# Shaking the due times of a list scheduler in a fused attention and MLP-mixer kernel

## The chip, the cores and the metric

The kernel runs on one core of a Trainium2 chip. The metric is the time of one execution in device microseconds (us). Before the change it is 423.1 us (median of 3 runs). Each experiment is timed beside the kernel before on the same chip.

## The reference

Eight batches of eight heads, 1024 positions, head size 64. Keys and values are first projected from 1024 positions to 64 (Linformer), then comes attention, then a token mixer with a residual and a channel mixer with a residual.

```python
k_proj = einsum('ks,bhsd->bhkd', E, k);  v_proj = einsum('ks,bhsd->bhkd', F, v)
attn = softmax(q @ k_proj.T / sqrt(64));  x = attn @ v_proj        # -> (8, 1024, 512)
h = relu(x.T @ w_tok1) @ w_tok2;          u = x + h.T              # 1024 -> 256 -> 1024
out = u + relu(u @ w_ch1) @ w_ch2                                  # 512 -> 1536 -> 512
```

## The kernel before

The kernel does not issue instructions as it goes. It records 2222 units of work ("jobs", each a few instructions of one engine or one transfer) with their dependencies, an estimated duration and a due time, and a list scheduler in the kernel's own code puts them in order and assigns the eight PSUM banks (the buffers that TensorE writes its products to). The program is then emitted in that order. So a due time decides only the order, not when something runs. The core of the scheduler:

```python
def plan(self):
    ...                                        # due times from those of the users
    for g in self.groups:                      # jobs that have to stay in sequence
        first = min(j.prio for j in g)
        for n, j in enumerate(g):
            j.prio = first + 0.01 * n
    ...
    while any(can.values()):
        ...                                    # for each engine: the jobs that can start
            t0 = min(c[0] for c in cands) + 0.02
            c = min((c for c in cands if c[0] <= t0), key=lambda c: (c[1], c[2]))   # due first
        ...
    return sorted(order, key=lambda j: j.at)
```

Transfers are on this schedule too, as jobs of one engine "DMA" that does one at a time, with a fixed duration. In the program GpSimd issues nearly all loads and stores, SyncE the transposes. A transpose of `u` (SBUF to SBUF, for the channel mixer) is entered with 3.5 us plus 2.0 of latency; those of batches 2 and later (batches are numbered from 0) get 3.0 us more. To keep loads and transposes apart, the kernel adds waits ("ties"). For batch b, four loads of 0.5 MB each bring k and v (first and second half of the heads); the transposes that take turns with them are the two of batch b - 2 (comments added):

```python
def load_kv(b):
    first, second = turned_u.get((b - 2, 0)), turned_u.get((b - 2, 1))
    jobs = load_group(b, "kv", first)     # k, k, v, v; all wait for the first transpose of u
    if second:
        tie(second, jobs[2])              # second transpose behind the first v
        tie(jobs[3], second)              # second v behind that transpose
        rest[b] = jobs[3:]                # put in a group with the q loads: v, q, q
```

If the loads go k, k, v, the second transpose waits for all three and runs alone.

The softmax here doesn't subtract the row's maximum and nothing guards it: scores larger than these inputs give would overflow.

## Time and profile before

| | before |
|---|---|
| time, median of 3 runs | 423.1 us |
| span of the profiled run | 421.2 us |
| TensorE (PE) busy | 98% |
| VectorE / ScalarE busy | 83% / 55% |
| stops of TensorE over 0.1 us after the first 38 us | 2.8 us in all |

TensorE decides the time. A "stop" here is the start of a matmul less the start of the one before it, less the columns of that earlier one at the full pace (0.109 us for 256 columns). The prediction shows the lines and how they are read.

### The profile page before, as it was taken

How to read it: one execution, taken by the hardware profiler on the slowest of the kernel's cores; microseconds unless marked ns; L12 is line 12 of the kernel's file. 1: busy time of each engine (PE TensorE's matmuls, PEld its weight loads, DVE VectorE, ACT ScalarE, POOL GpSimd, SP SyncE). 2: the span in 40 equal slices, each digit the busy share in tenths (PEclk: the TensorE clock that was granted, in tenths of full speed). 3: DMA queues.
4: the chain of work that ended last, by engine and by line, in shares of the span. 5: the costliest groups of instructions: out<-in, count | busy, mean ns of one | idle time of the engine just before them, and what ended most of it. 6: DMA issues, size and time to landing. Idle time of an engine off the chain costs nothing.

```text
span 421.2 us, 9421 instructions
## 1 busy us (share of the span) xinstructions
PE 412.1 (98%) x3838; PEld 347.7 (83%) x3838; DVE 348.0 (83%) x747; ACT 231.8 (55%) x444; POOL 66.2 (16%) x104
## 2 busy tenths in 40 slices
PE   7999999999999999999999999999999999999996
PEld 3587877688788888888798888888898899988885
DVE  2359969679679798988889899898988798997685
ACT  1858884475636546564645556655646645354530
POOL 8453220022003030022103020212100000010110
PEclk9999999999999999999999999999999999999999
DMA  9999999996975989398974989999760501250223
GB/s 166 207 201 206 207 206 164 225 177 140 216 145 103 195 133 235 64 186 141 207 163 94 191 139 224 163 200 179 153 146 0 152 27 76 50 151 2 102 100 103
DMA packets 96668, 62.48 MB, mean 148 GB/s; under 512 B 62064, under 2 KB 92272, under 8 KB 96624
## 3 DMA queue, kind: packets, MB, share of 16 engines
q0 software_dynamic: 34944, 45.09, 54.5%
q1 hardware_dynamic: 61056, 16.00, 21.6%
q10 hardware_dynamic: 624, 0.79, 0.7%
q8 instruction: 30, 0.49, 0.5%
q14 instruction: 14, 0.11, 0.1%
HBM read 59.24 MB, written 16.78 MB: 180 GB/s over the span
## 4 chain that ended last, share of the span: by engine, by line
PE 91%; DVE 4%; ACT 2%; DMA 1%; issue 0%; DVEq 0%
PE psum L1253 34%; PE psum L1144 33%; PE psum L848 4%; PE psum L484 4%; PE psum L597 3%; PE psum L964 3%; PE psum L656 2%; DMA o<-in_F_dram 1%; PE psum L620 1%; DVE u L1071 1%; PE psum L736 1%; PE psum L687 1%; PE psum L581 1%; PE psum L405 1%; PE psum L711 1%; PE psum L1032 1%
## 5 line engine op out<-in xcount | busy, mean ns | idle before, releaser
L1253 PEld LDWEIGHTS <-G 128*128 128x128 bf16 x1344 | 130.6, 98 | 19.7 <-issue 1.5
L1253 PE MATMUL psum<-wc_sb,G 128*128 128x256 bf16 x768 | 102.5, 273 | 0.5 <-ACT psum L1309 0.2
L1166 ACT ACTIVATE G<-psum 128x512 bf16<-128x512 f32 x96 | 57.3, 600 | 56.0 <-PE psum L1144 55.4
L1144 PEld LDWEIGHTS <-wc_sb 128*128 128x128 bf16 x768 | 73.8, 98 | 10.9 <-issue 0.6
L1253 PE MATMUL psum<-wT,G 128*128 128x256 bf16 x576 | 77.7, 273 | 0.1
L1180 DVE TENSOR_TENSOR G<-G 128x512 bf16<-128x512 bf16 (+1 forms) x140 | 69.5, 516 | 1.0
L1144 PEld LDWEIGHTS <-wT 128*128 128x128 bf16 x576 | 55.7, 98 | 9.0 <-issue 1.2
L1144 PE MATMUL psum<-uT,wc_sb 128*128 128x256 bf16 x384 | 57.7, 273 | 0.2 <-ACT psum L1187 0.2
L1144 PE MATMUL psum<-S,wc_sb 128*128 128x256 bf16 x384 | 57.6, 273 | 0.1
L1144 PE MATMUL psum<-S,wT 128*128 128x256 bf16 x384 | 55.6, 273 | 0.4 <-DVE S L781 0.4
L1287 POOL DMA_DIRECT2D out_dram<-o x30 | 16.4, 548 | 240.2 <-DVE o L1293 125.6
L1125 DVE CUSTOM_DVE_ANT_0 G<-psum,ub 128x512 bf16<-128x512 f32 x48 | 32.9, 685 | 15.3 <-PE psum L1144 15.1
L1172 ACT COPY ua<-psum 128x512 f32<-128x512 f32 x48 | 28.2, 588 | 30.1 <-PE psum L1144 29.7
L606 ACT ACTIVATE a<-psum 128x512 bf16<-128x512 f32 x64 | 36.4, 602 | 12.4 <-PE psum L597 11.8
L1293 DVE TENSOR_TENSOR o<-psum,u 128x512 f32<-128x512 f32 x55 | 37.5, 683 | 6.4 <-PE psum L1253 6.3
L1187 ACT COPY psum<-psum 128x512 f32<-128x512 f32 x48 | 27.8, 580 | 18.9 <-DVE G L1125 9.9
L1125 DVE CUSTOM_DVE_ANT_0 G<-psum,ua 128x512 bf16<-128x512 f32 x48 | 32.7, 682 | 5.0 <-ACT ua L1172 4.6
L1172 ACT COPY ub<-psum 128x512 f32<-128x512 f32 x48 | 28.2, 588 | 7.0 <-PE psum L1144 6.3
L1144 PE MATMUL psum<-uT,wT 128*128 128x256 bf16 x192 | 28.8, 273 | 0.1
L673 DVE TENSOR_TENSOR x_sb<-psum,rdn 128x512 bf16<-128x512 f32 x40 | 27.4, 686 | 0.6
L597 PE MATMUL psum<-qT,kT 128*128 128x512 bf16 x64 | 21.5, 380 | 0.6 <-ACT kT L549 0.6
L346 POOL DMA_DIRECT2D v_sb<-in_v_dram x18 | 13.5, 749 | 50.7 <-DMA uT<-u 48.0
(108 smaller groups left out, 547.2 us busy)
## 6 DMA issues: line engine op xcount, KB each, us to landing
out_dram<-o POOLq DMA_DIRECT2D x30, 512.0 KB, 4.2
k_sb<-in_k_dram POOLq DMA_DIRECT2D x14, 512.0 KB, 8.5
v_sb<-in_v_dram POOLq DMA_DIRECT2D x14, 512.0 KB, 10.3
q_sb<-in_q_dram POOLq DMA_DIRECT2D x14, 512.0 KB, 9.9
wc_sb<-in_moe_w_ch_dram POOLq DMA_DIRECT2D x6, 256.0 KB, 12.3
wc_sb<-in_moe_w_ch_dram POOLq DMA_DIRECT2D x4, 384.0 KB, 12.3
k_sb<-in_k_dram POOLq DMA_DIRECT2D x4, 256.0 KB, 6.8
v_sb<-in_v_dram POOLq DMA_DIRECT2D x4, 256.0 KB, 7.3
```

Source lines behind the costliest of these rows:

```text
L484: nc.tensor.matmul(t[0:KP, 0:hn], ET_sb[:, si, :], k_sb[:, hs, si, :], start=a, stop=z)
L597: lambda: nc.tensor.matmul(bank(bk), kT[:, h].rearrange("p c k -> p (c k)"), qT[:, h].rearrange("p j s -> p (j s)"), start=True, stop=True,),
L606: lambda: nc.scalar.activation(out=a_t[h // 2 % 2][:, h % 2], in_=bank(bk), func=ACT.Exp, scale=scale),
L673: lambda: nc.vector.tensor_tensor(out=x_sb[:, :, h * D : (h + 1) * D].rearrange("p (n c) d -> p n c d", n=2), in0=view()[:, :, :, 0:D], in ...
L1125: nc.vector._custom_dve(TENSOR_ADD_SAT, out=out, in0=in0, in1=in1, s0=FMAX, s1=0.0)
L1144: nc.tensor.matmul(t[:, c, :], w1_of(n, dd, 2 * m + c), a_of(j, n, dd), start=(n in (1, 7) and c == 0 and dd == 0), stop=(c == 1 and dd == 1),
L1166: lambda: nc.scalar.activation(out=G[:, n, cs], in_=view(src), func=ACT.Relu),
L1172: 512, lambda: nc.scalar.copy(out=dst, in_=view("y")), writes=[(name, s % 2)],
L1180: 512 * len(both), lambda: f(out=G[:, n, c], in0=G[:, a, c], in1=G[:, b, c]), ps=False,
L1187: 512, lambda: nc.scalar.copy(out=view("y"), in_=view("x")), takes=[bk["y"]],
L1253: nc.tensor.matmul(to, G[:, G_OF[n], cc, t * P : (t + 1) * P], w2_of(n, cc), start=(n in opens and (t == 0 or alone) and cc == 0), stop=(c ...
L1293: 512, lambda: nc.vector.tensor_add(out=dst, in0=view(src), in1=u_of(sh, dh)),
```

## The change

Its intent is to find a better order among many nearly equal ones: each due time is shaken by up to 0.8 us either way with a fixed sequence, and among many such shaken orders the one was kept whose planned time, averaged over randomly delayed transfers, is shortest. All of it but the three constants (`SHAKEN_FROM = -30.0`, `SHAKE = 1.6`, `SEED = 2441`):

```diff
             if j.prio > 1e8:
                 j.prio = max((d.prio for d in j.deps), default=0) + 2
+
+
+        for j in self.jobs:
+            if j.prio > SHAKEN_FROM:
+                j.prio += SHAKE * ((j.n * j.n * 7919 + j.n * SEED * 31 + SEED * SEED * 17) % 10007 / 10007 - 0.5)
         free = {}
```

The shaking comes after the groups, so it can also part what a group had put in sequence. All line numbers behind the change are 8 higher: L1152 is the L1144 of before, L1261 the L1253.

## The prediction

> **What bounds the kernel now.** I read the page first (busy shares, slices, chain of work), then TensorE's waits, then TensorE's timeline around its longest stops, then SyncE's and GpSimd's timelines for the transfers. The page's first lines and its chain:
>
> ```profile
> span 421.2 us, 9421 instructions
> PE 412.1 (98%) x3838; PEld 347.7 (83%) x3838; DVE 348.0 (83%) x747; ACT 231.8 (55%) x444; POOL 66.2 (16%) x104
> PE 91%; DVE 4%; ACT 2%; DMA 1%; issue 0%; DVEq 0%
> ```
>
> The reader is to see one engine, TensorE (PE), with work from end to end, and 91% of the chain that ended last on it. No other engine is near. So only two things can move the time: more or fewer matmuls, or more or fewer stops of TensorE. TensorE's own waits, complete:
>
> ```profile
> PE psum L433 <- DMA o<-in_F_dram: 1.5, 1, 1.5
> PE psum L405 <- DVE zero L309: 1.0, 1, 1.0
> PE psum L597 <- ACT kT L549: 0.6, 2, 0.4
> PE psum L1085 <- DVE u L1071: 0.5, 1, 0.5
> PE psum L1144 <- DVE S L781: 0.4, 1, 0.4
> PE psum L1253 <- ACT psum L1309: 0.2, 1, 0.2
> PE psum L1144 <- ACT psum L1187: 0.2, 1, 0.2
> PE psum L1253 <- DVE o L1293: 0.2, 1, 0.2
> ```
>
> Columns: total us, times, longest. The first five lie in the first 36 us, which the change hardly touches. Only the last three, 0.6 us, lie later. That understates the stops, because a matmul's row is longer than the step from one to the next. TensorE's timeline shows it:
>
> ```profile
> 229.33 0.60 PE L1144 MATMUL psum<-S,wc_sb 128*128 128x256 bf16 x4
> 230.15 0.60 PE L1144 MATMUL psum<-uT,wc_sb 128*128 128x256 bf16 x4 [0.22 <-ACT psum L1187]
> ```
>
> and the chain in order of time shows the undisturbed pace:
>
> ```profile
> 341.00 1.31 PE psum L1144 x12
> ```
>
> Twelve matmuls of 256 columns in 1.31 us are 0.109 us each. Four started at 229.33 should give way at 229.77; the next began at 230.15. So the stop was 0.38 us, although the view calls 0.22 of it idle. I took this surplus (start to start, less the columns at that pace) for every matmul. From 38 us to the last matmul, the surpluses that end with a wait on another engine and exceed 0.1 us are twelve: 0.39, 0.39, 0.38, 0.27, 0.23, 0.23, 0.18, 0.17, 0.15, 0.15, 0.12, 0.12, together 2.8 us. This is all that reordering can win after the head. 2.8 of 423 is 0.7%, so 2% faster (8.5 us) is out of reach.
>
> **What the Trainium skill says.** (1) "Perfetto Trace Analysis", introduction: matmul busy time says little of the distance to the roof, because matmuls are pipelined. The trace agrees: rows average 273 ns, starts are 109 ns apart. (2) "TensorE: Matmul & The Clock Gate", section "Wait — 56ns, not 53.3ns?": warm, start to start is columns / 2.4 GHz plus about 2.5 ns, so 109.2 ns for 256 columns. The trace agrees (109). (3) The same page, "Step-by-step: what each phase is for": matmuls stay in program order, only weight loads are pulled ahead. So one matmul whose operand is late holds all behind it, as at 229.77. (4) "DMA: Bandwidth & Descriptors", "Issuing engines are not separate DMA queues": all issuers share the 16 DMA engines. The trace agrees for slices 1 to 9, where the DMA digit stays at 9 with three queues at work.
>
> **The change part by part.** It removes and adds no instruction on TensorE: both programs have 7648 TensorE rows, 26 blank warm-up matmuls among them, and the dependencies between units of work are the same. It adds to every due time above -30 a fixed offset between -0.8 and +0.8 us, and a static list scheduler then picks another order and other PSUM banks. Of 904 TensorE units 677 stand elsewhere, by 3 places on average and 31 at most; of 741 VectorE units 554, of 443 ScalarE units 270. The first 18 TensorE units and the tail (last product and stores) stand as before, so the head, where the pace is lowest, and the last 4 us are unchanged.
>
> *Short loops.* The stops come where a product fills a PSUM bank, ScalarE or VectorE reads or reseeds it, and the next product on that bank waits, with too little other TensorE work laid between. At 229.33 and at 81.31 there is 0.44 us of such work and the stop is 0.39, so a ScalarE loop needs 0.83 us. That fits its parts: the last matmul ends 0.16 after its successor could start (273 - 109), the copy takes 0.58, and 0.09 is left for signalling.
>
> ```profile
> L1187 ACT COPY psum<-psum 128x512 f32<-128x512 f32 x48 | 27.8, 580 | 18.9 <-DVE G L1125 9.9
> L1293 DVE TENSOR_TENSOR o<-psum,u 128x512 f32<-128x512 f32 x55 | 37.5, 683 | 6.4 <-PE psum L1253 6.3
> ```
>
> The VectorE loop (0.68 instead of 0.58) needs 0.95: at 97 us there is 0.78 between and the stop is 0.17. I laid the matmuls of both orders end to end at the measured pace and counted these loops from 38 us of TensorE work on. Before, 6 loops are shorter than they need, short by 0.40, 0.39, 0.17, 0.17, 0.08 and 0.08, 1.29 us in all. The five stops found at such places measure 0.39, 0.39, 0.23, 0.23 and 0.17, 1.41 us, so the count is good to a tenth. After, 2 are too short: a VectorE loop with 0.44 between (short by 0.51) and one short by 0.08, 0.59 together. Loops under 1.0 us fall from 16 to 10, under 2.0 us from 353 to 336. Gain: 1.41 - 0.59 = about 0.8 us, all of it on TensorE, which sets the end.
>
> *Stops from queues on the evicting engines.* The other 1.4 us of the twelve are not short loops: the evicting engine was busy with something else (0.38 at 173 us, 0.30 in two stops at 210 us). No count tells what the new order makes of these. With fewer tight loops I take half, so a gain of 0.7 us.
>
> *Transfers.* Here the new order can lose. From the third batch on, loads and transposes take turns: k, k, v, then a transpose of u, then v, q, q. A late second v stops TensorE at the batch's key and value projection.
>
> ```profile
> 97.20 1.79 SPq L759 DMA_TRANSPOSE uT<-u  x1
> 101.96 0.74 POOL L346 DMA_DIRECT2D v_sb<-in_v_dram  x1 [1.34 <-DMA uT<-u]
> DMA to landing us min/median/max: 5.8/5.8/5.8
> 109.73 0.40 PE L484 MATMUL psum<-k_sb,ET_sb 128*64 128x512 bf16 x1
> ```
>
> These are SyncE's timeline, GpSimd's, the answer for that one load, and TensorE's timeline. The second v lands at 101.96 + 5.8 = 107.7, and the projection starts at 109.7: 2.0 us to spare, and about the same (2.1) in two further batches. The shaken order puts the first v ahead of both k in every second batch (frees the transpose some 5 us earlier, at 2.6 us a load) and the first q ahead of the second v (costs 2.6), and in the others moves the first v up one place. Meanwhile the projections move up in TensorE's order by 3.0, 0.9, 2.2, 4.1, 5.9 and 1.5 us in batches 2 to 7. What is left to spare, by those sums, is about 0.9 us in batch 2, 1 in batch 3 (where one qT transpose now goes ahead of uT, 2 to 3 us), 2.5 in batch 4, 0.5 in batch 5, and 2 or more after. None is negative, but three are thin, and transposes now overlap with loads, which slows both. I charge 0.4 us.
>
> Sum: -0.8 - 0.7 + 0.4 = -1.1 us, 423.1 to 422.0.
>
> **The rivals.**
> 1. *Nothing comes of it.* The stops of one kind go, others of the same size come, because 677 units moved and only the simplest loops were counted. For: of 2.8 us only half is explained by loops. Against: short loops fall at every limit I tried. Time 423.0.
> 2. *A load takes the place of the waits.* A second v lands late in batch 3 or 5 by 1 to 3 us, TensorE stands still, and the later work shifts. For: 0.5 to 1 us to spare, DMA busy at 9 tenths until about 95 us. Against: TensorE has no wait on a load after the head now, and the uT transpose before the second v starts earlier. Time 423.5 to 425.
> 3. *Nearly all stops go.* Queues on ScalarE and VectorE also thin out, no load is late. Against: the one VectorE loop with 0.44. Time 421.0.
>
> **Range and chances.** The middle is 422.0; rival 3 gives the low end, 421.0; rival 2 in its mild form the high end, 423.8. The part that cannot change (the matmuls, the head and the tail) is over 99% of the time and the runs before lie within 0.5 us, so within 2% is nearly certain. Slower by 8.5 us would take a load late in batch after batch: 1%. Faster by 8.5 us: 0.5%.
>
> **What would show it.** Right: TensorE busy stays 98%; the stops at 82, 173 and 229 us are gone; a new one of about 0.5 us stands at a VectorE eviction (L1293) near 88 us, before L1253; the surpluses over 0.1 us after 38 us sum to 1.2 to 1.6 instead of 2.8; the last v of a batch lands before its L484. Wrong: a TensorE wait on k_sb, v_sb or uT, or an L484 start that follows a landing; or the surpluses still sum to 2.8, which would be rival 1. A head longer or shorter than before (first 36 us) would mean that I misread what the shaking leaves alone.

## The result, and the profile after

The changed kernel takes 428.67 us (median of 4 runs, 428.11 to 430.18) against 423.22 for the kernel before. The ratio is 1.0133, interval 1.0106 to 1.016. The prediction said 422.0, with 423.8 as its high end: a gain of 1.1 us was foreseen, and a loss of over 5 was measured.

The head and the tail are as before. The first matmul that reads S and wT (the start of the channel mixer) begins at 35.6 us (35.9 before), and from the start of the last matmul to the end 4.2 us pass (4.3 before). Between these two marks lie 386.56 us, against 381.00. So 5.56 us are lost in the steady part. The page of the changed kernel, first lines and chain:

```profile
span 426.3 us, 9396 instructions
PE 412.5 (97%) x3823; PEld 348.6 (82%) x3838; DVE 348.5 (82%) x747; ACT 231.1 (54%) x444; POOL 66.3 (16%) x104
PE 86%; DMA 7%; DVE 4%; ACT 1%; issue 1%; POOL 1%; DVEq 0%; POOLq 0%
```

TensorE has the same work (412.5 us busy; the 15 matmuls fewer are records that the trace misses, as all 3838 weight loads are there), but DMA now holds 7% of the chain, 1% before. The list of TensorE's waits has a new first line:

```profile
PE psum L1152 <- DMA uT<-u: 4.6, 1, 4.6
```

One single wait, on a transfer that no line of the list named before: a transpose of `u`. TensorE's timeline shows where, first after the change, then the same reader before it:

```profile
99.90 0.60 PE L1152 MATMUL psum<-S,wT 128*128 128x256 bf16 x4
105.07 1.04 PE L1152 MATMUL psum<-uT,wc_sb 128*128 128x256 bf16 x4 [4.57 <-DMA uT<-u]
105.89 1.49 PE L1261 MATMUL psum<-wc_sb,G 128*128 128x256 bf16 x6
107.17 1.06 PE L856 MATMUL psum<-x_sb,wt_sb 128*128 128x256 bf16 x4
```

```profile
105.06 0.60 PE L1144 MATMUL psum<-uT,wc_sb 128*128 128x256 bf16 x4
```

Four matmuls from 99.90 should end their turn at 100.34; the reader of uT starts at 105.07, so the stop is 4.73 us. In the kernel before this reader stood at 105.06. The new order brought it forward by 4.7 us (105.06 to 100.34), and its operand did not follow. Note also that the six matmuls from 105.89 take until 107.17, which is 0.21 us each instead of 0.109. The view by windows of the changed kernel tells why; the third column from the right is the granted TensorE clock:

```profile
100.00:102.00 2.00, 0.50 (x6) 0.20 (x3) 2.00 (x6) 1.18 (x3) 0.00 (x0) 1.00 1.13 307
102.00:104.00 2.00, 0.00 (x0) 0.00 (x0) 1.33 (x3) 0.00 (x0) 0.00 (x0) 0.62 1.21 134
104.00:106.00 2.00, 0.93 (x5) 0.69 (x6) 0.43 (x1) 0.00 (x0) 0.38 (x1) 0.50 0.27 60
106.00:108.00 2.00, 2.00 (x11) 1.42 (x10) 0.00 (x0) 0.57 (x1) 1.87 (x3) 0.50 0.29 30
108.00:110.00 2.00, 2.00 (x15) 1.53 (x13) 0.00 (x0) 0.26 (x1) 0.00 (x0) 0.67 1.19 189
```

While TensorE stood, its clock was halved, from 102.5 to 109.3 by the clock records. From 105.07 to 109.3 it worked at half speed, which costs half of 4.26, 2.1 us. Stop and clock make 6.9 us. The measured loss is 5.56, so the rest of the order must have gained about 1.3.

Why was the transpose late? The answers for this one transfer, after and before:

```profile
L767 SPq DMA_TRANSPOSE uT<-u x1: 7402/7402/7402, 92.7 to 92.7; - x1
DMA to landing us min/median/max: 12.4/12.4/12.4
```

```profile
L759 SPq DMA_TRANSPOSE uT<-u x1: 1794/1794/1794, 97.2 to 97.2; - x1
DMA to landing us min/median/max: 4.2/4.2/4.2
```

It was issued 4.5 us earlier than before, and it landed 3.6 us later (105.0 against 101.4): 12.4 us under way instead of 4.2, and the issue alone held SyncE for 7.4 us instead of 1.8. GpSimd's timeline, after, shows what else was under way:

```profile
87.21 0.75 POOL L354 DMA_DIRECT2D v_sb<-in_v_dram  x1 [13.63 <-PE psum L1261]
87.95 0.77 POOL L354 DMA_DIRECT2D k_sb<-in_k_dram  x1
89.06 0.75 POOL L354 DMA_DIRECT2D k_sb<-in_k_dram  x1 [0.33 <-issue]
92.03 0.55 POOL L1295 DMA_DIRECT2D out_dram<-o  x1 [2.22 <-DVE rdn L640]
95.72 0.55 POOL L1295 DMA_DIRECT2D out_dram<-o  x1 [3.14 <-DVE o L1311]
```

The shaking put v ahead of both k. The transpose waits for that v alone, so it set out beside two k loads, and the new order also made two stores of outputs ready at just that time (before: at 100.07 and 110.73). By the landings, the k loads were in at 96.1 and 100.0, the stores at 102.5 and 103.9, the transpose last.

A third thing had moved. SyncE's timeline, after, has the first transpose of `u` behind one of q:

```profile
79.51 2.19 SPq L570 DMA_TRANSPOSE qT<-q_sb  x1
81.75 3.29 SPq L767 DMA_TRANSPOSE uT<-u  x1
```

Before, that transpose of `u` went first, at 79.96, and the one of q followed. All loads of batch 3 wait for it, so the first of them set out at 87.2 us instead of 85.5.

### The profile page after: what moved, and what is told of

The parts are those of the page before. It is cut to its first block, busy times and chain, and to the rows that moved or that the text cites. A ratio compares the mean times of both kernels' runs of the same rounds, so it can differ in the third digit from the quotient of the medians.

```text
span 426.3 us, 9396 instructions
## 1 busy us (share of the span) xinstructions
PE 412.5 (97%) x3823; PEld 348.6 (82%) x3838; DVE 348.5 (82%) x747; ACT 231.1 (54%) x444; POOL 66.3 (16%) x104
## 4 chain that ended last, share of the span: by engine, by line
PE 86%; DMA 7%; DVE 4%; ACT 1%; issue 1%; POOL 1%; DVEq 0%; POOLq 0%
PE psum L1261 33%; PE psum L1152 33%; PE psum L856 4%; PE psum L972 4%; DMA uT<-u 3%; DMA q_sb<-in_q_dram 3%; PE psum L492 3%; PE psum L605 2%; PE psum L664 2%; DMA v_sb<-in_v_dram 1%; DVE u L1079 1%; PE psum L695 1%; PE psum L719 1%; PE psum L628 1%; PE psum L744 1%
## 5 line engine op out<-in xcount | busy, mean ns | idle before, releaser
L1261 PEld LDWEIGHTS <-G 128*128 128x128 bf16 x1344 | 130.9, 98 | 19.7 <-issue 0.8
L1261 PE MATMUL psum<-wc_sb,G 128*128 128x256 bf16 x768 | 103.1, 274 | 0.5 <-DVE wait L1301 0.3
L1152 PEld LDWEIGHTS <-wc_sb 128*128 128x128 bf16 x768 | 74.2, 98 | 14.5 <-DMA uT<-u 4.8
L1261 PE MATMUL psum<-wT,G 128*128 128x256 bf16 x576 | 78.1, 273 | 0.5 <-ACT G L1174 0.2
L1152 PEld LDWEIGHTS <-wT 128*128 128x128 bf16 x576 | 55.9, 98 | 9.7 <-issue 1.0
L1152 PE MATMUL psum<-uT,wc_sb 128*128 128x256 bf16 x384 | 58.2, 274 | 4.6 <-DMA uT<-u 4.6
L1152 PE MATMUL psum<-S,wc_sb 128*128 128x256 bf16 x384 | 57.8, 273 | 0.1
L1152 PE MATMUL psum<-S,wT 128*128 128x256 bf16 x384 | 55.0, 273 | 0.5 <-DVE S L789 0.4
L1152 PE MATMUL psum<-uT,wT 128*128 128x256 bf16 x192 | 29.3, 276 | 0.1
L605 PE MATMUL psum<-qT,kT 128*128 128x512 bf16 x53 | 19.6, 379 | 1.0 <-ACT kT L557 0.7
```

The costliest lines, as they stand in the source:

```text
L605: lambda: nc.tensor.matmul(bank(bk), kT[:, h].rearrange("p c k -> p (c k)"), qT[:, h].rearrange("p j s -> p (j s)"), start=True, stop=True,),
L1152: nc.tensor.matmul(t[:, c, :], w1_of(n, dd, 2 * m + c), a_of(j, n, dd), start=(n in (1, 7) and c == 0 and dd == 0), stop=(c == 1 and dd == 1),
L1261: nc.tensor.matmul(to, G[:, G_OF[n], cc, t * P : (t + 1) * P], w2_of(n, cc), start=(n in opens and (t == 0 or alone) and cc == 0), stop=(c ...
```

## The experiments

The theory ("theory 1" below): the stop takes two things together, a transpose that shares the DMA engines with loads and stores, and its reader brought forward in TensorE's order. Rivals: the order of the loads alone ("theory 2"); the reader's place alone ("theory 3"); the late second v that the prediction had feared. All edits act on the finished plan, on single jobs around the loads of batch 3, so the rest of the program stays exactly as it was (TensorE's instructions are the same, in the same order, unless said). In the diffs, `put(a, b)` moves job a to just ahead of b, `put_after(a, b)` to just behind it, and `tied[a] = b` makes a wait for b. The jobs: 657 and 658 are the k loads, 659 the first v, 660 the second v, 915 the first q, 479 and 488 the first and second transpose of `u` of batch 1, 368 and 372 the stores.

**Loads k, k, v again (a_kkv).**

```diff
     plan = pl.plan()
+    put(657, 659)
+    put(658, 659)
```

> The changed kernel with one edit: in batch 3 the first three loads are issued k, k, v as before the change instead of v, k, k; the transpose of u (second half of batch 1) still waits for that v. TensorE order and everything else are the changed kernel's. In the changed kernel that transpose was issued at 92.65, took 12.4 us (4.2 before the change) and landed at 105.02, and TensorE stood still from 100.34 to 105.07. Theory 1 (the transpose is slow because it shares the DMA engines with the two k loads and two stores that are in flight): it now starts when v lands, at about 98 to 100, beside the stores alone, takes 4 to 7 us and lands at 103 to 105, so the stop is 3 to 4.7 us: 426 to 428 us, little gained by this edit alone. Theory 2 (the order of the loads alone is at fault): the stop goes to about 1 us and the time to about 422 to 423. Theory 3 (only the earlier place of the reader in TensorE's order counts, the transfers do not): the transpose takes as long as in the changed kernel.

Measured: 426.74 us against 423.69, ratio 1.0076 (1.0053 to 1.0099), correct. The transpose was issued at 99.4, took 4.5 us, landed at 103.9, and the stop was 3.1 us. Theory 2 fails: restoring the order of the loads recovers only about 2 of 5.5 us. Theory 3 fails in part: the transpose got fast again. The time is as theory 1 said. Of the traffic blamed, though, the stores (landed at 100.6 and 101.8) slowed this transpose hardly at all, and they had not held up the v before it either: that v took 9.8 us here and 9.7 without the stores (a_kkv_late2 below). The transpose is late here because its loads set out 2.2 us later than before (87.7 against 85.5), behind the first transpose of `u`.

**Stores behind the transpose (a_late, a_kkv_late), failed.**

```diff
+    put_after(368, 488)
+    put_after(372, 368)
+    tied[job[368]] = tied[job[372]] = job[488]
```

> The changed kernel with one edit: the two stores of outputs that were issued at 92.03 and 95.72, during the transpose, now wait until the transpose has landed. The loads stay v, k, k. Theory 1 (any traffic beside it slows the transpose): it is issued at about 92 as in the changed kernel, still beside two k loads (until about 98), takes 7 to 10 us instead of 12.4 and lands at 99 to 102; the stop is 0 to 2 us, 422 to 424.5 us. Theory 2 (load order alone): the stop stays over 4 us, 428 us. Theory 3 (place of the reader alone): no change, 428 us.

> Both edits together: loads k, k, v and the two stores behind the transpose, so that it runs alone as before the change. Theory 1: it is issued at about 97.5 to 98, takes 4.2 to 4.5 us and lands at about 102; the reader stands at 100.3, so a stop of about 1.7 us remains, and no loss of clock after it (the clock in this stage stays 1.0): 423 to 424 us. Theory 3 (place of the reader): the same 1.7 us is its whole share, against the 4.7 measured. If the time stays at 428, the transfers are not the cause.

Both gave a wrong result (436.1 and 437.6 us). My edit put the second store ahead of the addition that makes its data. They say nothing about the question, and were mended by leaving 372 where it is:

**The same, mended (a_late2 with loads v, k, k; a_kkv_late2 with loads k, k, v).**

```diff
+    put_after(368, 488)
+    tied[job[368]] = tied[job[372]] = job[488]
```

> a_late mended (there the second store was placed ahead of the addition that makes its data, hence its wrong result). The changed kernel, loads v, k, k as changed, but the two stores of outputs wait until the transpose of u has landed. Theory 1 (any traffic beside the transpose slows it): it is issued at about 92.5 and shares the DMA engines with the two k loads only; it takes 7 to 10 us instead of 12.4, lands at 99 to 102, the stop before its reader at 100.3 is 0 to 1.7 us: 421.5 to 424 us. Theory 2 (load order alone is at fault): over 4 us of stop, 428 us. Theory 3 (place of the reader in TensorE's order alone): 428 us.

> a_kkv_late mended in the same way: loads k, k, v and both stores behind the transpose, so it runs alone as before the change. Theory 1: the third load lands at about 97.7, the transpose takes 4.2 to 4.5 us and lands at about 102.1; the reader stands at 100.3, so 1.7 to 1.9 us of stop remain, which is the part of the earlier reader by itself: 423 to 424 us, with the granted clock from 100 to 110 us near 1.0. In a_kkv (stores not moved) the transpose took 4.5 and landed at 103.9. If it is slower than a_kkv (426.7), the stores were not what delayed the loads there.

Measured: 429.43 us (ratio 1.0136, 1.0119 to 1.0154) and 430.98 us (1.0171, 1.0156 to 1.0186), before 423.34; both correct. The times miss what every theory said, but the traces tell more than any other run. TensorE's waits in a_late2, then the answer for its transpose:

```profile
PE psum L495 <- DMA v_sb<-in_v_dram: 4.0, 1, 4.0
PE psum L1152 <- DMA uT<-u: 0.6, 1, 0.6
```

```profile
DMA to landing us min/median/max: 8.0/8.0/8.0
```

With the stores out of the way the transpose took 8.0 us instead of 12.4, landed at 101.4, and the stop before its reader fell from 4.73 to 0.76, as theory 1 expected. But behind it a second stop of 4.2 us appeared: the second v was now queued behind two stores and a q and landed at 113.4, while the projection that needs it stood at 109.0. A late v exists in the changed kernel too, only hidden: there the second v landed at 114.9 (106.36 + 8.5) and the projection, held back by the first stop, came at 114.7. It is not independent of the first: its tie lets it set out only after the transpose has landed, and then behind a q. The size of the second stop in these two runs is not that of the changed kernel, because my edit had also put the two stores ahead of that v. In a_kkv_late2 both stops show, 3.2 and 4.6 us. So batch 3 has two late transfers, one hidden behind the other. TensorE's wait for the first of them in a_kkv_late2:

```profile
PE psum L1152 <- DMA uT<-u: 3.0, 1, 3.0
```

There the transpose ran alone and took 4.2 us, and still landed at 103.9, 3.2 us after the reader could start. So a fast transpose is not enough. An estimate of the parts, from the landings: had it landed when it did before (101.4), the reader's new place (100.3) alone would have cost about 1.1 us of the 4.73; the later loads make that 3.1 to 3.2 (a_kkv, a_kkv_late2), and the order v, k, k with its company 4.73. Theory 1 left the later loads out.

**The suspected cost in the kernel before (b_vkk).** The same move the other way round: first v ahead of both k, TensorE's order of before.

```diff
+    put(659, 657)
```

> The kernel BEFORE with one edit, the suspected cost alone: in batch 3 the first v is issued ahead of both k, so the transpose of u starts some 5 us earlier, beside the two k loads. TensorE's order is that of before, where the reader of the transposed block starts at 105.06. Theory 1 (it takes the slow transpose and the earlier reader together): the transpose is issued at about 92, takes 6 to 10 us instead of 4.2 and lands by 102; no stop, 423.0 to 424 us, same as before. Theory 2 (load order alone is at fault): a stop of several us, 426 to 428 us.

Measured: 423.07 us against 423.34, ratio 0.9984 (0.9968 to 1.0001), correct.

```profile
L759 SPq DMA_TRANSPOSE uT<-u x1: 5175/5175/5175, 92.5 to 92.5; - x1
DMA to landing us min/median/max: 7.7/7.7/7.7
```

Beside two loads the transpose takes 7.7 us here as well, but it lands at 100.3, its reader stands near 105, and nothing is lost. The load order alone is not the cause. (The stores stayed behind the transpose here; the reverse test, the changed kernel with the reader alone put back, was not run.)

**The lost clock by itself (a_warm).** Twenty blank matmuls fill the stop.

```diff
+        if j.n == 570:                  # the reader of uT
+            for _ in range(20):
+                blank(banks[5])
+            pin()
         if j.eng == "PE":
```

> The changed kernel with 20 blank matmuls of 512 columns (4.3 us at 0.216 each) put into the stop ahead of the reader, into a PSUM bank that is free there (the reader's own, which it starts anew). The transfers and the stop's end at about 105 stay. In the changed kernel the granted clock was 0.50 from 104 to 108 us, and matmuls of 256 columns started every 0.214 us until about 108.5. If the lost clock is a cost of its own (theory: 2.0 to 2.3 us of the 7), TensorE keeps its clock and the time falls to 426.2 to 426.8 us. If the half clock comes from elsewhere, the time stays at 428.7 or rises.

Measured: 428.36 us, ratio 1.0114 (1.0099 to 1.0129), correct. The windows of a_warm:

```profile
104.00:106.00 2.00, 1.62 (x10) 0.82 (x9) 0.43 (x1) 0.00 (x0) 0.00 (x0) 1.00 0.53 83
106.00:108.00 2.00, 2.00 (x21) 1.78 (x19) 0.00 (x0) 0.57 (x1) 1.88 (x3) 1.00 0.14 20
```

The clock stays at 1.00 and 21 matmuls fit in two microseconds instead of 11, so idleness did halve the clock. But the time hardly falls, and my expectation of 426.5 was wrong. TensorE, now faster, arrives at the projection earlier and waits there for the second v (1.3 us in its trace); the transpose was also 0.5 us later. The 2.1 us of half clock were real work time, but most of it lay beside the wait for that v.

**The second v alone (a_v_only).**

```diff
+    put(660, 915)
```

> The changed kernel with the second v of batch 3 ahead of the first q, nothing else. Theory: the v lands some 2.5 us earlier than in the changed kernel (114.9), but the stop before the transposed block at 100 to 105 comes first and stays at 4.7 us with its lost clock, and the v had just landed by the time the projection came: 428 to 428.7 us, no gain. Rival (the late second v is the main cost): 424 to 426 us.

Measured: 428.53 us, ratio 1.0109 (1.0092 to 1.0126), correct. As expected, no clear gain: the stop before uT's reader stays (5.5 us in this run). The rival that the second v is the main cost fails.

**Second v ahead, stores behind it, transpose left beside the k loads (a_late_v).**

```diff
+    put(660, 915)
+    put_after(368, 660)
+    put_after(372, 368)
```

> The changed kernel's loads v, k, k and the transpose behind the first v, as changed; but the second v goes ahead of the q loads, and the two stores behind it. In a_late2 the transpose so placed took 8.0 us, landed at 101.4 and left a stop of 0.8, and the second v, queued behind two stores and a q, landed at 113.4 and stopped TensorE for 4.2 us. Theory (two thin transfers, each hidden behind the other): the stop of 0.8 stays, the v lands at about 108, and the time is 422.5 to 423.5 us, though the transpose is still slow. Rival (the transpose must go first): 426 us or more.

Measured: 423.89 us, ratio 1.0003 (0.9986 to 1.0021), correct. The loss against the kernel before is gone, though the transpose still takes 8.4 us (stop 1.1 us). The time is a little above the expected 422.5 to 423.5; the trace has a new stop of 1.15 us at 124 us, on the transpose of the keys (kT): the q loads had been pushed back, and the transposes behind them too.

**The transpose first (a_turn_first).** Issue the second transpose directly behind the first, ahead of all three loads; second v ahead of the q loads, stores behind it.

```diff
+    put(488, 659)
+    tied[job[488]] = job[479]
+    for n in (657, 658, 659):
+        tied[job[n]] = job[488]
+    put(660, 915)
+    put_after(368, 660)
+    put_after(372, 368)
```

> The changed kernel, but in batch 3 the transpose of u (second half) goes directly behind that of the first half, ahead of the three loads (which then wait for it or follow in the queue), the second v goes ahead of the q loads, and the two stores go behind that v. TensorE's order is the changed kernel's. Theory 1: the transpose is issued at about 84 to 87, lands by 91, long before its reader at 100.3; no stop there and no loss of clock; the second v lands at about 104 to 105, before the projection at 108. 421 to 422 us, that is 6 to 7 us under the changed kernel and 1 to 2 under the kernel before. If the expected gain of 1 to 1.5 us from fewer short waits was not real, 423 us. If the second v lands late, a stop of 1 to 3 us before the projection.

Measured: 422.36 us (421.95 to 422.81) against 423.69, ratio 0.9967 (0.995 to 0.9985), correct. The transpose:

```profile
L767 SPq DMA_TRANSPOSE uT<-u x1: 1771/1771/1771, 87.0 to 87.0; - x1
DMA to landing us min/median/max: 4.2/4.2/4.2
```

It runs alone, lands at 91.2, and TensorE waits for no transfer in the steady part. Between the two marks named above lie 379.57 us, 7.0 less than in the changed kernel and 1.43 less than before. TensorE's order is untouched, so the transfers made the whole loss. The edit moves the transpose, the second v and the stores at once; whether the transpose first would do alone was not run.

**Control: the transpose first in the kernel before (b_first).**

```diff
+    put(488, 657)
+    tied[job[488]] = job[479]
+    for n in (657, 658, 659):
+        tied[job[n]] = job[488]
```

> Control: the kernel BEFORE with the transpose of u ahead of the three loads of batch 3, as in a_turn_first. TensorE's order is that of before, which waits for no transfer there. Theory (the gain of a_turn_first over before, 0.3%, is that of TensorE's order with fewer short waits): 423.0 to 423.8 us, ratio 0.999 to 1.002. Rival (the gain comes from the earlier transpose itself): 422.4 us, ratio 0.997.

Measured: 423.88 us against 423.34, ratio 1.0007 (0.9987 to 1.0026), correct. Its steady part is 380.87 us, that of before 381.00. An early transpose by itself is worth nothing here. The moves of the second v and of the stores were not tried in the kernel before, but its TensorE waits for no transfer after the head (the prediction shows the list), so they had no such wait to remove. What a_turn_first wins over before is then TensorE's new order.

**Two short waits less (a_best).** In a_turn_first I took 0.50 us at 88.32 and 0.42 at 114.16 for the longest short waits. One unit of other work goes into each. (The second reading was wrong: the trace misses one 512-column matmul of L744 there, 0.22 us of work, whose weight load it has. The wait was 0.20 us.)

```diff
     ...                       # as a_turn_first
+    put_after(365, 493)
+    put(744, 546)
```

> a_turn_first with two units of TensorE work moved by one place, at the two longest short waits that its trace still shows: at 88.32 (0.50 us, a VectorE eviction with 0.44 us of work in between) a product of another block goes between, and at 114.16 (0.42 us) the second half of a token product. Theory: the two waits fall to under 0.15 us, TensorE stays the bound, so the time falls by 0.6 to 0.9 us against a_turn_first's 422.4: 421.5 to 421.9, ratio to before about 0.995. If short waits do not add up on the path, it stays at 422.4.

Measured: 421.54 us (421.27 to 421.94) against 423.34, ratio 0.9952 (0.9937 to 0.9967), correct. TensorE's timeline at the first place, in a_turn_first and in a_best:

```profile
88.14 0.39 PE L628 MATMUL psum<-vb,a 128*128 128x130 bf16 x4
88.87 0.81 PE L1261 MATMUL psum<-wc_sb,G 128*128 128x256 bf16 x6 [0.34 <-DVE wait L1301]
```

```profile
88.23 0.60 PE L1152 MATMUL psum<-uT,wc_sb 128*128 128x256 bf16 x4
88.73 0.71 PE L1261 MATMUL psum<-wc_sb,G 128*128 128x256 bf16 x5
```

The gap is filled with work. Both waits are gone from the trace, but two others came up in that execution (0.32 us on a v load at 47 us, 0.24 at 89.5), and the steady part of the profiled runs is the same (379.56 and 379.57). Their spans differ by 0.5 us, all of it before the first mark (35.95 against 36.48 us), where the edit changes nothing. The two kernels ran on different chips, and their intervals overlap. So it is shown that a_best beats the kernel before, by 0.5%; that it beats a_turn_first is not shown, though the time fell where it was expected.

## Why the prediction was wrong, and where it was right

- **What bounds the kernel, and that nothing is added on TensorE: right.** Head and tail are unchanged within 0.4 us, the work is the same. (Both programs, when built, hold 3838 matmuls and 3822 weight loads.)
- **Short loops and queues, -0.8 and -0.7 us: right in their sum.** Without the wait for uT and the half clock behind it, the stops over 0.1 us after 38 us fall from 2.8 to 1.4 us (0.50, 0.27, 0.20, 0.20, 0.12, 0.10), inside the 1.2 to 1.6 foreseen. Gaps of 0.22 us that are only a 512-column matmul missing from the trace are left out or taken off. The stops at 82, 173 and 229 us are gone, and the one new VectorE stop stands where it was said to, 0.50 us at 87.4 before L1261. With the transfers repaired (a_turn_first) the steady part is 1.43 us shorter than before, against 1.5 foreseen; by the ratio of the times the gain lies between 0.6 and 2.1 us. How it splits between the two is not shown. If the 0.50 is the only loop left over 0.1 us, loops gave 0.9 and the rest 0.5, an estimate; that half of the rest would go was a guess in the prediction, and its coming near was in part luck.
- **The step that failed: "I charge 0.4 us" for transfers.** The charge turned out to be 7.0 us (changed kernel against a_turn_first); the trace shows 6.9 of it as 4.73 of standing and 2.1 of half clock. It failed in two ways. First, "What is left to spare" was worked out for one transfer and one user only, the second v and the projection. The transposed `u` has a user too. Its reader moved forward by 4.7 us, and before the change the transpose had landed only 3.6 us ahead of it (101.4 and 105.06). Second, "(frees the transpose some 5 us earlier" was booked as a gain. An earlier start beside two loads and two stores meant 12.4 us instead of 4.2, so it landed 3.6 us later, and the second v, which waits for it, set out 4.4 us later (106.36 against 101.96) where the sum for batch 3 left 1 us to spare. The sentence that transposes now overlap with loads, "which slows both", was there, but without a size; the size can be read from a_late2, b_vkk and a_late_v: 8.0, 7.7 and 8.4 us beside two loads, 12.4 with the two stores as well. For the loads the runs do not show it: the last of the three took 9.75 us beside the transpose (b_vkk) and 9.73 without it (before).
- **Rival 2 was the right family with the wrong member and size.** A transfer of batch 3 did take the place of the waits, and TensorE stood still, but the first one was uT, not v, and the time was 428.7 and not 423.5 to 425. The second v was late as well, hidden behind the first stop: it landed at 114.9, and without stop and half clock the projection would have come at about 107.8 instead of 114.7 (an estimate: 6.9 us less).
- **The clock was not in the sum at all.** The wait was taken to cost its own length. The page "TensorE: Matmul & The Clock Gate" of the Trainium skill says in "What's actually happening" that the clock halves after an idle window of about 3.4 us. The trace agrees in the length of the window (half clock from 102.5 to 109.33, which is twice 3.41 us), but not in the idleness: TensorE had stood for only 2.2 us when the clock fell. In the end the clock cost little: with it kept (a_warm) the steady part is 0.6 us shorter, as the wait for the second v took its place.
- **The citation on shared DMA engines** was backed with the DMA digit of 9 and "three queues at work". That reading is wrong: three queues moved data only in the first 10 us, and from 10 to 70 us nearly all packets were those of one queue, GpSimd's. What points to sharing here is the transpose, 4.2 us alone and 7.7 to 12.8 in company.
- **The intent of the change explains the miss in part.** Orders were chosen by a plan in which a transpose takes a fixed time and the DMA does one transfer at a time. On the chip this transpose took 1.8 to 3 times as long in company (7.7 to 12.8 us against 4.2). The plans can be computed without the chip from the two kernels. For this transpose they say: landing at 101.4 and reader at 102.7 us before the change, 96.9 and 98.4 after. The chip had 101.4 before, as planned, and 105.0 after, 8.1 us late. The plan also entered the two stores behind the transpose (105.4 and 106.9); on the chip they set out at 92.0 and 95.7. And of the 14 transposes of `u`, 12 are planned with 3.0 us of extra latency; the two of batch 1, of which this is one, are not. That this lack let the order through is argued, not tested. How large the random delays in that choice were, and whether another seed would have avoided it, no run here shows.

## What to carry to other kernels

When work is reordered under a bound engine, check the room of every transfer that feeds it, each at its own first reader, and not just of the one that was thin before. A transfer that sets out earlier but in company can land later than one that waits and runs alone (here 105.0 against 101.4), so a schedule that models transfers one by one is only as good as the waits that keep them apart. And after repairing one late transfer look for the next: two waits in a row can hide each other, so that a repair alone seems worthless, as a_v_only did here. Before calling a gap a stop, check with the weight loads that no matmul is missing from the trace.

## What the Trainium skill lacked or had wrong

- "DMA: Bandwidth & Descriptors", "Rules for kernel authors", says that a transpose next to ordinary DMAs needs nothing. For correct results that held here, but not for time, and it gives no figure for a transpose in company: alone the SBUF transpose of `u` landed after 4.2 to 4.3 us, beside two 0.5 MB loads after 7.7 to 8.4, beside two loads and two stores after 12.4 to 12.8.
- The same page, "Issuing engines are not separate DMA queues", calls the time that a sequencer takes to initiate a DMA usually small relative to the DMA itself. For this transpose it was not: the issuing instruction held SyncE for 7.4 of 12.4 us in company, and for 1.8 of 4.2 alone.
- "TensorE: Matmul & The Clock Gate", "What's actually happening", gives an idle window of about 3.4 us for the half clock. Less was enough: in the changed kernel TensorE worked until 100.34 and the clock was halved from 102.50, 2.2 us later. In a_kkv a stop of 3.12 us halved the clock from 103.6 to 107.0, 2.8 us after it began, but in a_kkv_late2 one of 3.18 us at the same place did not. What decides between the two, these runs do not show.
